# Silu as one ScalarE activation in the first layer's gate of a retention and two-layer feed-forward kernel

## The chip, the cores and the metric

One Trainium2 chip, one of its cores. The metric is the device time of one execution of the whole program, in microseconds (us), given as the median of the runs. Five engines matter: TensorE (PE in the profile, with its weight loads as PEld), VectorE (DVE), ScalarE (ACT), GpSimd (POOL) and SyncE (SP, which here issues DMAs). Each engine works through its own queue in order. An instruction that has to wait for another engine holds up all that stands behind it in its queue.

## The reference, cut to what matters

Retention over 4 batches of 8 heads (576 positions, 64 dimensions a head) gives 2304 tokens of 512 values. Two feed-forward layers follow. Each has a hidden width of 2048, and everything is float32.

```python
def _moe_ref(x, w_in, w_out):            # first layer, "layer 0"
    h = x @ w_in                         # (2304, 512) @ (512, 2048)
    g = h * (1.0 / (1.0 + np.exp(-h)))   # the gate: silu(h)
    return (g @ w_out).astype(np.float32)

def _moe2_ref(x, w_in, w_out):           # second layer, "layer 1"
    h = x @ w_in
    r = np.maximum(h, 0.0)
    g = r * r
    return (g @ w_out).astype(np.float32)
```

## The kernel before, in words

Every float32 product is made of three fp32r matmuls: each operand is split into a rounded high part and the rest (`xh`/`xl`, `wh`/`wl`, `gh`/`gl`), and `mm3` (line 74) adds high times high, high times low and low times high.

The tokens are cut into five blocks of 512, 384, 384, 512 and 512 (`BLOCKS`). The order of the work is written out by hand. The main loop (lines 504 to 529) goes through 160 steps: layer 0 with its five blocks, then layer 1 with its five blocks, each block in 16 steps `f` of 128 hidden columns. A step `i` emits, in this order:

- `gemm1(i)`: 12 matmuls from `x` and the weights into the PSUM tile `ph` (two buffers). It puts `gate(i)` on the list `later`.
- First half: `conv_to` (weight conversion, below) where weights are still to be converted, and then `flush`, which emits all that stands in `later`. What these emit may put new entries on the list, for the next flush.
- Second half: `conv_to`, `flush`, and then `gemm2(i-2)` (`LAG` is 2): 12 matmuls from `gh`, `gl` and the weights into the four PSUM tiles `acc`.
- After either half in layer 0, at evenly spaced places, a part of the retention of the next block (`scores`, `values`), whose own DVE and ACT work goes onto `later` too.

In the kernel before, the gate of step `i` takes three flushes. First half of step `i`: ACT computes Sigmoid from `ph` into `sg` (line 380), DVE multiplies `ph` by it into `sg` (line 381). Second half of step `i`: ACT rounds `sg` into `gh` (line 388). First half of step `i+1`, behind that half's weight conversion: DVE makes `gl = sg - gh` (line 389). `gemm2(i)` on PE in step `i+2` needs both. Layer 1 has its own gate (lines 383 and 384), with the same split.

The weights come as 512 KB pieces in a 64-bit layout and are converted on the chip: ACT lines 101, 102 (`conv_a`) and 121 (`conv_c`), DVE lines 107 to 109 (`conv_b`) and 125 (`conv_d`). For layer 0 this runs during the start and the 16 steps of block 0, one piece in each half step. For layer 1 it runs from the last block of layer 0 into the first steps of layer 1. After each `conv_b` SP is given the load of a later piece into the buffer that this `conv_b` frees.

Before layer 1 can begin with a block, `load_x2` (lines 435 to 444) loads the first layer's result back (SP), copies it four times on ACT (`xh`, line 442) and subtracts it four times on DVE (`xl`, line 443). The first `load_x2` is emitted at the end of step `f = 8` of the last block of layer 0, the second at the end of step `f = 4` of the first block of layer 1.

Before the start a Sigmoid of one element (`dummy`, line 455) runs on ACT.

Of the kernel before, what the change touches and what calls it, by code (L numbers as in the profile page):

```python
# [9 lines left out]
ACTF = mybir.ActivationFunctionType  # L10
# [28 lines left out]
def kernel(  # L39
# [16 lines left out]
    nc = tc.nc  # L56
# [72 lines left out]
    later = []  # L129
# [44 lines left out]
    dummy = cp.tile([128, 1], F32, name="dummy")  # L174
# [184 lines left out]
    def gemm1(layer, j, f):  # L359
        n = BLOCKS[j]  # L360
        ph = ps_g.tile([128, 512], F32, tag="g", name="ph")[:, 0:n]
        wh, wl = wt[layer, f]
        xh, xl = x_t[j] if layer == 0 else late["x", j]
        for k in range(KD):
            w0 = slice(k * 128, k * 128 + 128)
            mm3(
                ph,
                [(wh[:, w0], xh[:, k, 0:n]), (wh[:, w0], xl[:, k, 0:n]), (wl[:, w0], xh[:, k, 0:n])],
                first=k == 0,
                last=k == KD - 1,  # L370
            )
        later.append(lambda: gate(layer, j, f, ph))

    def gate(layer, j, f, ph):
        n = BLOCKS[j]
        s = gp.tile([128, 512], F32, tag="sg", name="sg", bufs=2)[:, 0:n]
        gh = gp.tile([128, NBMAX], F32R, tag="gh", name="gh")[:, 0:n]
        gl = gp.tile([128, NBMAX], F32R, tag="gl", name="gl")[:, 0:n]
        if layer == 0:
            nc.scalar.activation(s, ph, ACTF.Sigmoid)  # L380
            nc.vector.tensor_mul(s, ph, s)  # L381
        else:
            nc.scalar.activation(s, ph, ACTF.Relu)  # L383
            nc.vector.scalar_tensor_tensor(s, ph, 0.0, s, op0=ALU.max, op1=ALU.mult)  # L384
        g_t[layer, j, f] = (gh, gl)

        def split():
            nc.scalar.copy(gh, s)  # L388
            later.append(lambda: nc.vector.tensor_sub(gl, s, gh))  # L389

        later.append(split)

    def gemm2(layer, j, f):
        n = BLOCKS[j]
# [57 lines left out]
    for _ in range(WARM):  # L452
        mm(warm[:, 0, 0:256], zero[:, 0:128], zero[:, 0:256], start=True, stop=True)
    nc.vector.memset(dummy, 0.0)
    nc.scalar.activation(dummy, dummy, ACTF.Sigmoid)
    for u in range(n_start):
        if u == 0:
            new_raw(u)
# [45 lines left out]
    for i in range(len(seq) + LAG):  # L504
        if i < len(seq):
            layer, j, f = seq[i]
# [79 lines left out]
```

## Time and profile before

| | us |
|---|---|
| median of 3 runs | 898.37 (897.97 to 899.33) |
| the profiled execution | 897.14 |
| its span, first to last instruction | 895.40 |
| PE busy | 862.8 (96%) |
| DVE busy | 427.6 (48%) |
| ACT busy | 327.1 (37%) |
| POOL busy | 72.8 (8%) |
| mean granted clock of PE | 0.982 of full speed |

The profile is one execution, so its times are compared with 897.14, of which 1.74 lie outside the span. Busy shares are means over stages that have different limits. The start (about 0 to 40 us) prepares the first block. Block 0 of layer 0 follows, to about 145, then the other blocks of layer 0, to about 490, and layer 1 to the end. An idle engine costs time only where PE waits for it or where the end of the program does.

### The profile page before, as it was taken

The page shows a single profiled execution, that of the slowest core. Times are in us where ns is not written, and L with a number is a line of the kernel's source. Part 1 is how long each engine was busy: PE and PEld are TensorE (multiplying, and loading weights), DVE is VectorE, ACT ScalarE, POOL GpSimd, SP SyncE. Part 2 cuts the span into 40 slices and gives each one's busy share as a digit, 9 for nine tenths or more (in the row PEclk, how much of TensorE's full clock was granted, in tenths as well). Part 3 has the DMA queues.
Part 4 walks back from the last instruction along what each step waited for, and adds up shares of the span by engine and source line. Part 5 has one row for each costly group of instructions (what it writes and reads, how often), then busy time and mean ns, then how long its engine had stood idle before and what let it go on. Part 6 is the DMA issues. An engine that isn't in the chain of part 4 may idle for free.

```text
span 895.4 us, 14028 instructions
## 1 busy us (share of the span) xinstructions
PE 862.8 (96%) x5930; PEld 739.8 (83%) x5930; DVE 427.6 (48%) x722; ACT 327.1 (37%) x594; POOL 72.8 (8%) x105
## 2 busy tenths in 40 slices
PE   6698979999999999999999989999999999999998
PEld 5576758999999888888878878889999888888886
DVE  3899995333443333335767776632242233223222
ACT  3576663222222322225556555432232223222221
POOL 5210111111122021100000000000000000000000
PEclk8699999999999999999999999999999999999999
DMA  9445532111211213002343433020020020001001
GB/s 355 175 140 191 181 127 95 48 48 48 84 49 48 84 48 118 1 1 95 120 139 118 142 131 115 2 83 1 1 83 1 0 83 1 1 0 48 1 1 47
DMA packets 21662, 68.27 MB, mean 76 GB/s; under 512 B 2400, under 2 KB 4192, under 8 KB 21216
## 3 DMA queue, kind: packets, MB, share of 16 engines
q1 hardware_dynamic: 17280, 59.91, 19.5%
q10 hardware_dynamic: 4320, 7.47, 2.3%
q8 instruction: 46, 0.75, 0.3%
q14 instruction: 16, 0.13, 0.0%
HBM read 57.93 MB, written 9.44 MB: 75 GB/s over the span
## 4 chain that ended last, share of the span: by engine, by line
PE 82%; DVE 2%; DMA 1%; issue 0%; ACT 0%; SPq 0%; ACTq 0%
PE acc L74 40%; PE ph L74 39%; PE Q L301 2%; DMA xr<-x 1%; PE P L250 1%; PE P L255 1%; DVE xl L443 0%; DVE t L108 0%; DVE gl L389 0%; DVE t L109 0%; DVE t L107 0%; DVE wl L125 0%; PE Q L317 0%; ACT xh L442 0%; SPq L92 0%
## 5 line engine op out<-in xcount | busy, mean ns | idle before, releaser
L74 PE MATMUL ph<-xh,wh 128*128 128x512 f32 (+1 forms) x640 | 238.1, 372 | 5.6 <-ACT xh L335 5.6
L74 PE MATMUL ph<-xl,wh 128*128 128x512 f32 (+1 forms) x640 | 236.4, 369 | 0.0
L74 PE MATMUL ph<-xh,wl 128*128 128x512 f32 (+1 forms) x640 | 236.3, 369 | 0.0
L384 DVE SCALAR_TENSOR_TENSOR sg<-ph,sg 128x512 f32<-128x512 f32 (+1 forms) x80 | 51.0, 638 | 195.3 <-ACT sg L383 195.3
L74 PEld LDWEIGHTS ph<-xh,wh 128*128 128x128 f32 x640 | 120.8, 189 | 24.0 <-ACT xh L335 5.8
L74 PEld LDWEIGHTS ph<-xl,wh 128*128 128x128 f32 x640 | 120.7, 189 | 16.8 <-DVE xl L336 0.4
L74 PEld LDWEIGHTS ph<-xh,wl 128*128 128x128 f32 x640 | 120.7, 189 | 15.2
L74 PE MATMUL acc<-gl,wh 128*128 128x512 f32 (+1 forms) x320 | 120.2, 376 | 9.6 <-DVE gl L389 9.4
L389 DVE TENSOR_TENSOR gl<-sg,gh 128x512 fp32r<-128x512 f32 (+1 forms) x160 | 103.5, 647 | 52.9 <-ACT gh L388 52.6
L388 ACT CAST gh<-sg 128x512 fp32r<-128x512 f32 (+1 forms) x160 | 92.3, 577 | 91.2 <-DVE sg L384 51.5
L381 DVE TENSOR_TENSOR sg<-ph,sg 128x512 f32<-128x512 f32 (+1 forms) x80 | 50.9, 636 | 148.7 <-ACT sg L380 148.7
L74 PE MATMUL acc<-gh,wh 128*128 128x512 f32 (+1 forms) x320 | 120.5, 377 | 0.0
L383 ACT ACTIVATE sg<-ph 128x512 f32<-128x512 f32 (+1 forms) x80 | 44.5, 556 | 207.9 <-PE ph L74 207.5
L74 PE MATMUL acc<-gh,wl 128*128 128x512 f32 (+1 forms) x320 | 119.0, 372 | 0.0
L74 PE MATMUL acc<-wh,gl 128*128 128x512 f32 x288 | 112.8, 392 | 2.8 <-DVE gl L389 2.8
L74 PE MATMUL acc<-wl,gh 128*128 128x512 f32 x288 | 112.6, 391 | 0.0
L74 PE MATMUL acc<-wh,gh 128*128 128x512 f32 x288 | 112.0, 389 | 0.0
L380 ACT ACTIVATE sg<-ph 128x512 f32<-128x512 f32 (+1 forms) x80 | 44.3, 554 | 159.0 <-PE ph L74 159.0
L74 PEld LDWEIGHTS acc<-gl,wh 128*128 128x128 f32 x320 | 60.8, 190 | 21.3 <-DVE gl L389 13.9
L74 PEld LDWEIGHTS acc<-gh,wh 128*128 128x128 f32 x320 | 60.6, 189 | 8.7
L74 PEld LDWEIGHTS acc<-gh,wl 128*128 128x128 f32 x320 | 60.9, 190 | 7.4
L74 PEld LDWEIGHTS acc<-wh,gl 128*128 128x128 f32 x288 | 54.1, 188 | 14.6 <-DVE gl L389 3.2
(50 smaller groups left out, 738.0 us busy)
## 6 DMA issues: line engine op xcount, KB each, us to landing
wr<-w SPq DMA_DIRECT2D x64, 512.0 KB, 3.5
raw<-att SPq DMA_DIRECT2D x34, 512.0 KB, 5.3
x<-y ACTq DMA_DIRECT2D x12, 256.0 KB, 2.5
xr<-x SPq DMA_DIRECT2D x3, 1024.0 KB, 5.5
out<-y SPq DMA_DIRECT2D x10, 256.0 KB, 2.1
out<-y ACTq DMA_DIRECT2D x7, 256.0 KB, 2.3
x<-y ACTq DMA_DIRECT2D x8, 192.0 KB, 1.9
xr<-x SPq DMA_DIRECT2D x2, 768.0 KB, 5.3
```

Source lines behind the costliest of these rows:

```text
L74: mm(o, a, b, start=first and i == 0, stop=last and i == n - 1)
L250: mm(o, dims(u, a, e, b, 768), dims(u, a, e, b, 0), start=True, stop=True)
L255: mm(o, toks(u, a, e, b, 256), toks(u, a, e, b, 512), start=True, stop=True)
L301: mm(w, a, b, start=e not in started, stop=last)
L380: nc.scalar.activation(s, ph, ACTF.Sigmoid)
L381: nc.vector.tensor_mul(s, ph, s)
L383: nc.scalar.activation(s, ph, ACTF.Relu)
L384: nc.vector.scalar_tensor_tensor(s, ph, 0.0, s, op0=ALU.max, op1=ALU.mult)
L388: nc.scalar.copy(gh, s)
L389: later.append(lambda: nc.vector.tensor_sub(gl, s, gh))
```

## The change

The gate of layer 0 loses its product on DVE. ACT's activation from `ph` into `sg` is Silu in place of Sigmoid. `split` is called at once in layer 0, so that the rounding into `gh` stands directly behind the Silu in ACT's queue, and the subtraction that makes `gl` goes out with the next flush (second half of step `i`) and not with the one after that. Layer 1's gate is as it was. The one-element activation before the start is Silu too.

```diff
         if layer == 0:
-            nc.scalar.activation(s, ph, ACTF.Sigmoid)
-            nc.vector.tensor_mul(s, ph, s)
+            nc.scalar.activation(s, ph, ACTF.Silu)
         else:
             nc.scalar.activation(s, ph, ACTF.Relu)
             nc.vector.scalar_tensor_tensor(s, ph, 0.0, s, op0=ALU.max, op1=ALU.mult)
@@
             nc.scalar.copy(gh, s)
             later.append(lambda: nc.vector.tensor_sub(gl, s, gh))
 
-        later.append(split)
+        if layer == 0:
+            split()
+        else:
+            later.append(split)
@@
     nc.vector.memset(dummy, 0.0)
-    nc.scalar.activation(dummy, dummy, ACTF.Sigmoid)
+    nc.scalar.activation(dummy, dummy, ACTF.Silu)
```

## Rows read from the trace of the kernel before

**Rows 1.** Stretches: busy us (instructions) of each engine, granted clock, DMA share, GB/s.

```profile
40.00:140.00 100.00, 90.16 (x688) 69.98 (x687) 93.75 (x156) 66.43 (x115) 14.99 (x17) 0.98 0.46 153
140.00:450.00 310.00, 310.00 (x2732) 277.68 (x2731) 125.12 (x220) 92.23 (x172) 40.00 (x58) 1.00 0.19 63
450.00:465.00 15.00, 13.13 (x51) 10.37 (x50) 11.05 (x19) 9.39 (x17) 0.00 (x0) 0.89 0.33 114
...
535.00:890.00 355.00, 355.00 (x1649) 304.40 (x1648) 121.40 (x198) 101.99 (x185) 0.00 (x0) 1.00 0.08 27
```

**Rows 2.** PE's waits, 40 to 140: us in total, times, longest us.

```profile
PE acc L74 <- DVE gl L389: 7.5, 8, 2.4
PE Q L301 <- DVE S L286: 2.1, 1, 2.1
```

**Rows 3.** PE's waits from 440 to 540, same columns.

```profile
PE acc L74 <- DVE gl L389: 4.7, 2, 2.8
```

**Rows 4.** DVE, groups by line, 40 to 140: busy us, mean ns; idle before, releaser.

```profile
L381 DVE TENSOR_TENSOR sg<-ph,sg 128x512 f32<-128x512 f32 x15 | 10.2, 682 | 3.0 <-ACT sg L380 3.0
L389 DVE TENSOR_TENSOR gl<-sg,gh 128x512 fp32r<-128x512 f32 x14 | 10.1, 721 | 0.0
```

**Rows 5.** DVE's timeline in block 0: start us, us, instruction.

```profile
54.11 0.68 DVE L381 TENSOR_TENSOR sg<-ph,sg 128x512 f32<-128x512 f32 x1
54.71 0.68 DVE L257 TENSOR_TENSOR rf<-P,cs 128x512 f32<-128x512 f32 x1
...
93.73 0.42 DVE L107 TENSOR_SCALAR t<-t 128x512 int32<-128x512 int32 x1
...
133.18 0.41 DVE L286 TENSOR_TENSOR S<-P,dS 128x256 f32<-128x256 f32 x1
```

**Rows 6.** PE's timeline in block 0, idle time before in brackets.

```profile
83.86 0.50 PE L74 MATMUL acc<-gl,wh 128*128 128x512 f32 x1 [2.38 <-DVE gl L389]
...
84.67 0.60 PE L74 MATMUL acc<-gl,wh 128*128 128x512 f32 x1
...
88.31 0.40 PE L74 MATMUL ph<-xl,wh 128*128 128x512 f32 x1
...
90.84 0.39 PE L74 MATMUL acc<-gh,wh 128*128 128x512 f32 x1
...
97.15 0.50 PE L74 MATMUL acc<-gl,wh 128*128 128x512 f32 x1 [0.48 <-DVE gl L389]
...
133.74 1.09 PE L301 MATMUL Q<-raw,S 64*64 64x64 f32 x30 [2.08 <-DVE S L286]
```

**Rows 7.** ACT's timeline around the first load_x2.

```profile
443.31 0.60 ACT L380 ACTIVATE sg<-ph 128x512 f32<-128x512 f32 x1 [1.80 <-PE ph L74]
...
452.44 2.18 ACT L442 CAST xh<-xr 128x512 fp32r<-128x512 f32 x4 [6.38 <-DMA xr<-x]
```

**Rows 8.** DVE's timeline there.

```profile
453.09 2.50 DVE L443 TENSOR_TENSOR xl<-xr,xh 128x512 fp32r<-128x512 f32 x4 [6.07 <-ACT xh L442]
455.51 0.68 DVE L389 TENSOR_TENSOR gl<-sg,gh 128x512 fp32r<-128x512 f32 x1
...
459.10 0.68 DVE L389 TENSOR_TENSOR gl<-sg,gh 128x512 fp32r<-128x512 f32 x1
```

**Rows 9.** PE's timeline there.

```profile
456.24 0.50 PE L74 MATMUL acc<-gl,wh 128*128 128x512 f32 x1 [1.87 <-DVE gl L389]
...
456.58 0.48 PE L74 MATMUL acc<-gh,wl 128*128 128x512 f32 x1
...
460.23 0.39 PE L74 MATMUL acc<-gh,wl 128*128 128x512 f32 x1
```

**Rows 10.** ACT, groups by line, 40 to 140, columns as in rows 4.

```profile
L101 ACT ACTIVATE t<-wr 128x512 f32<-128x512 f32 x26 | 17.5, 675 | 4.9 <-DMA wr<-w 2.2 <-DVE gl L389 1.7 <-DVE wl L125 1.0
...
L121 ACT CAST wh<-t 128x512 fp32r<-128x512 f32 x28 | 17.4, 621 | 18.6 <-DVE t L109 18.3
...
L380 ACT ACTIVATE sg<-ph 128x512 f32<-128x512 f32 x15 | 8.8, 590 | 1.2 <-PE ph L74 1.2
```

**Rows 11.** ACT's only table load in the whole span, by line.

```profile
L455 ACT ACT_TABLE_LOAD x1 | 1.3, 1283 | 0.7 <-PEq L576 0.7
```

## The prediction

> **What bounds the kernel now.** I read the busy times by stretch first, to see where PE is not full. From 140 to 450 and from 535 to 890 it is busy all the time at full clock [rows 1]. Nothing that DVE or ACT save there can move the end. In the 100 us from 40 to 140, block 0 of layer 0, PE is busy for 90.2 while DVE is busy for 93.8: DVE converts a piece of the weights in each half step and makes the gates between. ACT has 66.4 there. PE's waits in that stretch, read next, are 7.5 us in eight waits for `gl` and 2.1 in one for the retention's state `S`, all made by DVE [rows 2]. The third view is PE's waits around the two `load_x2`: 4.7 us in two waits for `gl`, one of 1.9 at 456 and one of 2.8 [rows 3, 9]. So what can be won is some 14 us in places that can be named, and in each of them PE waits for DVE.
>
> A wait costs more than its length where the granted clock falls behind it. After the 2.38 us wait that ends at 83.86, nine matmuls from 84.67 to 88.31 take 3.64 us, 0.40 each, and from 88.31 to 90.84 eleven take 2.53, 0.23 each [rows 6]: the lower level of 1.2 GHz cost 1.6 us. After the wait at 456.24 nine matmuls take 3.65 us (456.58 to 460.23) [rows 9], again 1.6 too much, and that stretch has a mean clock of 0.89 [rows 1].
>
> **The change part by part.** *The product goes.* One product holds DVE's queue for 0.60 us (from 54.11 to 54.71, where the next one starts) [rows 5], though it is listed at 0.68. From 40 to 140 there are 15 [rows 4]. Two come after the `S` that ends PE's last wait (133.18), 13 before it: 13 x 0.60 = 7.8 us. In addition DVE sat idle for 3.0 us in front of products, until the Sigmoid was there [rows 4]. Of that I take back 2.2: in the two places where a retention copy stands ahead of the gate on ACT, DVE's next `wl` waits for ACT's `wh`, which now stands behind Silu and `gh`, and I leave 0.4 for each. So DVE reaches this `S` 7.8 + 2.2 = 10.0 us earlier, and PE could begin the matmuls behind it at 133.7 - 10.0 = 123.7 [rows 6]. PE alone, without its waits (7.5 + 2.1) and without the slow 1.6, would be there at 133.7 - 11.2 = 122.5. The later one decides: block 0 gives 10.0, with 7.8 (none of the idle time comes back) and 11.2 as its ends.
>
> *Does `gl` still hold PE up?* It leaves with the second half's flush, so it no longer stands behind the next half's conversion. The tightest place that I find is step 7. There the conversion that stood ahead of `gl` begins at 93.73 [rows 5]; `gl` now takes that place, 8 x 0.60 earlier for eight products and 1.4 for the idle time up to there: 87.5, done at 88.2. PE, had it not waited, would want it at 97.15 less the gl waits up to there (0.4, 0.3, 0.9, 0.3, 2.4 and 0.5, of which rows 6 show the two last) and 1.6 of clock, at 90.7. That leaves 2.5 us, so these eight waits go, and the clock's fall behind the 2.38 with them.
>
> *Silu in Sigmoid's place.* No row shows Silu. The nearest is Sigmoid in the same place, 590 ns; the costliest activation of the same size there is the one of line 101, 675 ns, from SBUF [rows 10]. I take 590. The ends are nothing below it (the operands and the size stay) and 675, which is 15 x 0.085 = 1.3 us on an engine that has 33.6 us free in that stretch [rows 1], hidden.
>
> *`gh` is moved forward on ACT*, directly behind the Silu. It no longer waits for a product. What is queued behind it is the second half's `wh` and the first step of the next conversion, which come one cast (616 ns for the same form, near L121's 621 [rows 10]) later; they have waited for DVE 18.3 us in all [rows 10], so that is the cover, and if it is gone DVE's `wl` is late (first rival). No DMA is moved; the weight loads that SP issues after each `conv_b` come earlier with DVE, and no retention load changes its place. In blocks 1 to 4 the same parts are worth nothing, since PE never waits there [rows 1].
>
> *The first `load_x2`.* Its four copies wait for the load until 452.44 on ACT, and its four subtractions until 453.09 on DVE [rows 7, 8]. The `gl` of step 8 stood behind them and came at 455.51 [rows 8]; PE waited 1.87 for it [rows 9]. Now that `gl` is emitted a half step earlier, before `load_x2`, right after the Silu that takes the place of the Sigmoid at 443.31 [rows 7]. It is some nine us early. What is late next is the `gl` of step 9: at 459.10 now [rows 8], less the `gl` and the product that stood between it and the subtractions (2 x 0.60), 457.9, done at 458.6. PE wants it 24 matmuls of 0.23 after 454.4 (456.24 - 1.87), at 459.9. So this wait goes with its slow clock: 1.9 + 1.6 = 3.5, and if the clock falls there anyway, 1.9. The second `load_x2` lies in layer 1, whose gate is not touched: its 2.8 stays.
>
> **The sum.** 10.0 + 3.5 = 13.5 us off the profiled execution's 897.1 (span 895.4 and 1.7 outside it). The median of the runs is 1.2 above that execution; taken off the median, 898.4 - 13.5 = 884.9. The ends of this case are 7.8 + 1.9 = 9.7 (888.7) and 11.2 + 3.5 = 14.7 (883.7), and if the second `load_x2` should win its 2.8 too, 880.9.
>
> **The rivals.** *The saving is eaten by the new order on ACT.* `wh` of the second half now waits for PE's `ph`, for Silu and for `gh`; DVE's `wl` waits for it, and everything of DVE behind that. If this takes 0.6 a step, DVE runs block 0 at its old pace, and all that is left is that `gl` goes out one conversion earlier (93.73 to about 96.4, as PE was released at 97.15 [rows 5, 6], 2.7 us), at most once over the block. With the 3.5 of `load_x2` that is 3.5 to 6.2, about 893.5. For it: DVE and PE have nearly the same amount of work (90 each after the change), so waits on either side add. Against it: ACT is free a third of the time, and by the places worked out above PE is the one that runs ahead.
>
> *Slower: table loads on ACT.* The trace has one table load, 1283 ns, before the first Sigmoid, and none between Sigmoid and the other functions of ACT [rows 11]. If Silu could not share a table with the Abs of line 101, each step of block 0 would need two loads, 28 in the 14 steps of the stretch: 35.9 us. ACT would have 66.4 + 35.9 = 102.3 us of work where PE and DVE have about 90, and with half of its 18.3 us of waits for DVE kept, 111.5. That is 11.5 more than now; less the 3.5 of `load_x2`, about 906. It decides from more than (90 - 66.4) / 14 = 1.7 us of loads a step, so one load a step would be hidden and two are not. Against it: Sigmoid, Abs, Copy and Relu ran here on one load. The Trainium skill, "ScalarE: Activation LUTs", section "Table sets: the hidden batching unit", speaks of this danger: functions come in sets around one costly function, and each change of set is a load. It also says that relu, copy and abs are in every set as filler. The trace agrees for Sigmoid's set; no run here shows Silu's. The page prices a switch at 2.66 us with a drain that no row here shows; an estimate by that would put 74 us on ACT, some 41 us of them beyond the present stretch, about 940.
>
> *No change.* The waits for `gl` turn into waits for other things of DVE, `S` above all, and the clock falls at the same places. This would need DVE not to gain by work that it no longer has. About 898. That Silu is made of two ACT instructions, so that the change isn't what it says, would put 15 x 0.59 = 8.9 us on ACT, 75 of about 90: hidden, the forecast's time.
>
> **How the numbers follow.** Forecast (881 to 889) 0.72; eaten on ACT (889 to 896) 0.17; no change 0.05; slower 0.06. Faster by over 0.2% (1.8 us, about what a measurement of this kernel can tell from none) is 0.72 + 0.17 = 0.89, same 0.05, slower 0.06. The range goes from 881.5, which leaves a little of the forecast's far end out, to 893.5, the middle of the first rival.
>
> **What would show it.** In the changed profile: DVE without line 381's product, some 10 us less busy in block 0; one table load; Silu near 590 ns; PE's waits for `gl` in block 0 near nothing and one of 1 us or so for `S`, its matmuls of `values` begun near 124; no low clock near 85; at the first `load_x2` no wait for `gl`, at the second still 2.8. The prediction is wrong if ACT shows more than one table load, if PE's waits for `gl` in block 0 stay above 4 us in all, or if a wait for `wl` or `wh` appears that was not there.

## The result, and the profile after

The changed kernel takes 888.83 us (median of four executions, 887.45 to 890.08), beside 898.85 (897.97 to 899.37) for the one before: a ratio of 0.9889, with a 95% interval of 0.9869 to 0.9909. That is 10.0 us off, where 13.5 were forecast. It ends inside the stated range, 3.9 us above the predicted time.

The profiled execution is the longest of the four: 890.08 us, span 888.3. It is 7.06 us under the profiled execution before (897.14), so an account made from the two traces has to come to 7.1 and not to 10.0. The four executions lie in two groups, two at 887.5 to 888.0 with a mean granted clock of 0.988 and 0.990, two at 889.7 to 890.1 with 0.983. The profiled one is of the second group, and below it can be seen where its clock falls.

The stretches of the changed kernel (columns as in rows 1):

```profile
40.00:140.00 100.00, 92.92 (x711) 75.30 (x710) 88.90 (x145) 68.38 (x119) 15.12 (x17) 0.97 0.45 154
140.00:450.00 310.00, 310.00 (x2730) 277.53 (x2730) 92.51 (x166) 95.78 (x178) 37.56 (x58) 1.00 0.19 65
450.00:465.00 15.00, 15.00 (x67) 12.40 (x67) 11.95 (x21) 10.71 (x19) 0.00 (x0) 1.00 0.44 140
```

PE's waits from 36 to 136 (us in total, times, longest), against [rows 2], and then from 430 to 540, against [rows 3]:

```profile
PE ph L74 <- ACT xh L335: 6.4, 1, 6.4
PE Q L301 <- DVE S L286: 4.7, 2, 4.1
PE ph L74 <- ACT sg L380: 1.9, 2, 1.3
PE acc L74 <- DVE gl L388: 0.4, 1, 0.4
...
PE acc L74 <- DVE gl L388: 2.7, 1, 2.7
```

The first row is the wait for the block's first operand, ahead of the first matmul of block 0; it belongs to the start and was there before too. In block 0 the eight waits for `gl`, 7.5 us, have become one of 0.4. The wait for `S` has grown from 2.1 to 4.1 (with a small second one 4.7), and two waits of a new kind stand there, for the Silu that frees `ph`, the PSUM tile that `gemm1` writes. At the first `load_x2` nothing is left. At the second the wait is 2.7, as it was.

PE's timeline where the last wait of block 0 ends:

```profile
126.77 1.51 PE L301 MATMUL Q<-raw,S 64*64 64x64 f32 x23 [4.07 <-DVE S L286]
...
129.52 0.79 PE L74 MATMUL acc<-gh,wh 128*128 128x512 f32 x1
...
132.13 0.39 PE L74 MATMUL acc<-gh,wh 128*128 128x512 f32 x1
```

From 129.52 to 132.13 six matmuls take 2.61 us, 0.43 each, where 0.23 is usual: PE is at 1.2 GHz behind this wait (the stretch's granted clock is 0.51, below), as it was behind the one of [rows 6] that ends at 83.86. The matmuls of `values` in front of them take 2.75 us (126.77 to 129.52). From 126.77 to 132.13 that is 5.36 us together; in the kernel before, the same matmuls took 3.04, from 133.74 [rows 6] to here:

```profile
136.78 0.39 PE L74 MATMUL acc<-gh,wh 128*128 128x512 f32 x1
```

So the low clock behind this wait costs 2.3 us.

The granted clock of this stretch (columns as in rows 1):

```profile
125.00:130.00 5.00, 3.23 (x65) 3.15 (x66) 4.84 (x8) 1.66 (x4) 2.76 (x3) 0.51 0.00 0
```

Each kernel's first matmul of block 0, before and after:

```profile
35.23 0.80 PE L74 MATMUL ph<-xh,wh 128*128 128x512 f32 x1 [5.58 <-ACT xh L335]
```

```profile
35.98 0.79 PE L74 MATMUL ph<-xh,wh 128*128 128x512 f32 x1 [6.40 <-ACT xh L335]
```

So the account of the two profiled executions is this. The start was 0.75 longer; in the second run of the same kernel (below) block 0 began at 35.34, so that is not the change's doing. From the first matmul of block 0 to the `values` behind the last `S` PE took 98.5 us before (35.23 to 133.74 [rows 6]) and takes 90.8 now (35.98 to 126.77): 7.7 won. The low clock behind it gives 2.3 back. The first `load_x2` wins 1.9 of wait and 1.6 of clock. The second loses 1.4, as the experiment there shows. That makes 7.7 + 3.5 - 0.75 - 2.3 - 1.4 = 6.8 of the 7.06; the rest is in no row that was read.

### The profile page after: what moved, and what is told of

Same layout as the page of the kernel before. It is cut to its first block, busy times and chain, and to the rows that moved or that the text cites. A ratio compares the mean times of both kernels' runs of the same rounds, so it can differ in the third digit from the quotient of the medians.

```text
span 888.3 us, 13947 instructions
## 1 busy us (share of the span) xinstructions
PE 860.0 (97%) x5930; PEld 741.0 (83%) x5930; DVE 381.0 (43%) x642; ACT 327.9 (37%) x594; POOL 70.5 (8%) x105
## 4 chain that ended last, share of the span: by engine, by line
PE 84%; DVE 1%; DMA 1%; ACT 0%; issue 0%; SPq 0%; ACTq 0%
PE acc L74 41%; PE ph L74 40%; PE Q L301 2%; PE P L250 1%; PE P L255 1%; DMA xr<-x 1%; DVE xl L445 0%; PE Q L317 0%; DVE t L108 0%; DVE t L109 0%; DVE t L107 0%; DVE wl L125 0%; DVE gl L388 0%; ACT sg L382 0%; ACT xh L444 0%
## 5 line engine op out<-in xcount | busy, mean ns | idle before, releaser
L74 PE MATMUL acc<-gl,wh 128*128 128x512 f32 (+1 forms) x320 | 118.2, 369 | 0.4 <-DVE gl L388 0.4
L74 PEld LDWEIGHTS acc<-wh,gl 128*128 128x128 f32 x288 | 54.4, 189 | 14.6 <-DVE gl L388 3.2
L74 PEld LDWEIGHTS acc<-wh,gh 128*128 128x128 f32 x288 | 54.5, 189 | 10.5
```

The source lines that it names most:

```text
L74: mm(o, a, b, start=first and i == 0, stop=last and i == n - 1)
```

## The experiments

All of them were timed beside the kernel before, in two groups on two chips. The changed kernel's second run, the late split, the early split alone and the two states in one flush shared 898.25 us for it; the two table loads, `gl` twice and the two with the early split in layer 1 shared 898.44. Where one of the second group is set against the changed kernel's 888.82, that goes across the groups; the ratios to the kernel before give the same differences within 0.3 us.

**The changed kernel once more.**

> The changed kernel as it is, for the comparisons of this group, and to see how much its time moves between executions: 887 to 890 us. Theory (DVE's work up to the last state S sets block 0): the wait of PE for S of about 4 us near 127 is there again. Rival (it was an accident of one execution): it is under 1 us.

Measured: 888.82 us (887.70 to 890.07), ratio 0.9894, interval 0.9880 to 0.9908. The wait for `S` in its trace is 4.07 us again, so it is no accident of one execution.

**Silu alone, the split where it was.** From the changed kernel:

```diff
-        if layer == 0:
-            split()
-        else:
-            later.append(split)
+        later.append(split)
```

> Silu in place of Sigmoid and product, but the split where it was before (gh in the second half, gl in the next step). Theory (block 0 is won by the work taken off DVE, the first load_x2 by gl's earlier place): block 0 wins what the changed kernel wins there, the last S starts near 126, and the first load_x2 keeps its wait of 1.9 us, with or without 1.6 us of slow clock: 1.9 to 3.5 us behind the changed kernel, 890.5 to 892.5. Rival (the earlier place of gl does it all): 896 to 898.5, waits for gl in block 0 as before.

Measured: 887.42 us (885.74 to 888.06), ratio 0.9875, interval 0.9862 to 0.9889. That is 1.4 under the changed kernel in the same group; the two intervals overlap, so it is not shown to be faster, but it is clearly not slower, and my theory had 2 to 3.5 us more. The rival's 896 to 898.5 is off as well. PE's waits of this kernel, 36 to 140 and then 400 to 540:

```profile
PE acc L74 <- DVE gl L388: 3.5, 6, 1.0
PE Q L301 <- DVE S L286: 1.6, 1, 1.6
...
PE acc L74 <- DVE gl L388: 2.9, 1, 2.9
```

Block 0 wins as much as in the changed kernel: from the first matmul to the `values` behind the last `S` it takes 90.34 us. Its waits are many and short where those of the changed kernel are one long one, and no low clock follows them. The surprise is the second stretch. Its one wait is that of the second `load_x2`; the wait at the first is gone, although `gl` of step 8 still stands behind the subtractions there. How, its timelines show: SP's issue of the load, ACT's Silu of step 8, and DVE.

```profile
435.18 0.36 SPq L437 DMA_DIRECT2D xr<-x  x1
```

```profile
435.14 0.60 ACT L380 ACTIVATE sg<-ph 128x512 f32<-128x512 f32 x1 [2.53 <-PE ph L74]
```

```profile
441.42 2.50 DVE L442 TENSOR_TENSOR xl<-xr,xh 128x512 fp32r<-128x512 f32 x4 [4.45 <-ACT xh L441]
443.83 0.68 DVE L388 TENSOR_TENSOR gl<-sg,gh 128x512 fp32r<-128x512 f32 x1
```

Against the kernel before, where SP's issue is

```profile
446.92 0.38 SPq L438 DMA_DIRECT2D xr<-x  x1
```

and the Sigmoid of step 8 starts at 443.31 [rows 7]: the load used to leave 3.6 us after that Sigmoid began, and leaves 0.04 us after the Silu began here. It stands in SP's queue behind a weight load that waits for a `conv_b` of DVE, and DVE no longer waits for the gate before that `conv_b`. The load, the subtractions and `gl` come so much earlier that PE no longer waits.

**The early split alone.** From the kernel before, Sigmoid and product kept:

```diff
-        later.append(split)
+        if layer == 0:
+            split()
+        else:
+            later.append(split)
```

> Sigmoid and the product on DVE stay, and the split alone comes early (gh directly behind the product, gl in the second half). Theory: DVE has all its work up to the last S, so S starts near 133 as before and block 0 wins under 2 us; the first load_x2 loses its wait: 893 to 896. Rival (order alone): 888 to 891. In either case ACT, with gh queued ahead of the second half's wh, now waits for DVE's product; if that costs, the last S comes later than 133.

Measured: 895.37 us (894.53 to 897.54), ratio 0.9966, interval 0.9952 to 0.9979, as my theory had it. PE's waits, 36 to 140 and then 400 to 540:

```profile
PE ph L74 <- DVE sg L381: 5.7, 5, 2.5
...
PE Q L301 <- DVE S L286: 4.7, 2, 4.0
...
PE acc L74 <- DVE gl L389: 2.9, 1, 2.9
```

The waits for `gl` in block 0 are gone here too, but waits of about the same size in all for the product (it frees `ph`) and for `S` stand in their place, and block 0 takes 97.8 us from the first matmul to the `values`, 0.7 less than before. The wait at the first `load_x2` is gone, this time because `gl` of step 8 leaves ahead of the subtractions; the load itself leaves as late as ever, 3.6 us after the Sigmoid of step 8. So there are two causes, and either of them alone removes that wait.

**Two table loads a step.** From the changed kernel:

```diff
         if layer == 0:
             split()
+            if j == 0:
+                nc.scalar.activation(dummy, dummy, ACTF.Sigmoid)
```

> The changed kernel with a Sigmoid of one element behind each gh in block 0 of layer 0, so that Silu's table has to be loaded again in every step of that block: if the two functions lie in two tables, 2 loads a step, 32 more in all at 1.28 us, 41 us of ACT's time. Theory (the slower rival's price): ACT becomes what bounds block 0, as the prediction worked it out, and the kernel ends near 906 (900 to 915), slower than the one before. Rival (ACT's waits for DVE, 16 us in block 0, take most of the loads up): 889 to 897. If one table holds both functions, there are no more loads and nothing changes.

Measured: 904.62 us (903.63 to 907.48), ratio 1.0071, interval 1.0048 to 1.0095: 15.8 us slower than the changed kernel, and within 1.4 us of the 906 that the prediction gave this rival. ACT's groups (busy us, mean ns), and the wait of DVE that the loads make:

```profile
L393 ACT ACT_TABLE_LOAD x16 | 20.5, 1283 | 0.3
L380 ACT ACT_TABLE_LOAD x16 | 20.5, 1283 | 0.3
```

```profile
DVE wl L125 <- ACT wh L121: 17.4, 13, 3.2
```

Silu and Sigmoid lie in different tables, a change between them is 1283 ns each time, and 32 of them, 41 us of ACT's time, cost the kernel 15.8. ACT is busy for 97.1 of the 104 us from 36 to 140, and its wait for DVE's conversion is down to 0.8. In the changed kernel ACT runs Silu, Abs, Copy and Relu on one load, so this rival did not come true; its price came out, if not by its working: block 0 takes 107.6 us from the first matmul to the `values`, 9.0 more than before, where the price had 11.5, with half of ACT's 18.3 us of waits for DVE's conversions kept. ACT's timeline in this run shows what one change costs:

```profile
64.52 0.62 ACT L387 CAST gh<-sg 128x512 fp32r<-128x512 f32 x1
65.16 1.28 ACT L393 ACT_TABLE_LOAD   x1
66.45 0.20 ACT L393 ACTIVATE dummy<-dummy 128x1 f32<-128x1 f32 x1
```

The load begins 0.02 us after the cast ends, and the activation 0.01 after the load: 1.3 us in all. The Trainium skill, "ScalarE: Activation LUTs", section "Table sets: the hidden batching unit", says that relu, copy and abs are in every set; the one load of the changed kernel agrees for Silu's. Its price of 2.66 us with a drain, in the section "What ACT_TABLE_LOAD costs", is not what these rows show; the 1283 ns of the load itself is.

**The two states in one flush.** From the changed kernel:

```diff
             new_state(u, 0, P)
-            later.append(lambda: new_state(u, 1, P))
+            new_state(u, 1, P)
```

> The changed kernel, with both states of a retention step made in one flush on DVE, so that the second S no longer stands behind a weight conversion of 2.5 to 3 us; DVE waits about 0.7 to 1 us for POOL's dS between the two. Theory (S is what PE waits for last in block 0): the wait of 4.1 us before the matmuls of values near 127 shrinks to 0.5 to 2, and the slow clock behind it goes: 2 to 5 us faster than the changed kernel, 884 to 887. Rival (DVE's total work sets the pace, so any wait saved for S comes back as a wait for gl): within 1 us of the changed kernel.

Measured: 888.01 us (887.04 to 888.16), ratio 0.9882, interval 0.9869 to 0.9896. It is 0.8 under the changed kernel, too little to tell apart: the rival's time and not the theory's, though the rival's mechanism is hardly seen (the waits for `gl` are 0.8 us in all, where they were 0.4). PE's waits from 36 to 140:

```profile
PE Q L301 <- DVE S L286: 2.2, 1, 2.2
PE ph L74 <- ACT sg L380: 2.1, 2, 1.8
PE acc L74 <- DVE gl L388: 0.8, 2, 0.5
```

The wait for `S` is half as long, but the low clock follows it all the same. The granted clock is 0.50 from 127 to 130, and the matmuls of `values` take 2.71 us, as in the changed kernel (2.75); only the matmuls behind them are spared, all but the first:

```profile
126.86 1.82 PE L301 MATMUL Q<-raw,S 64*64 64x64 f32 x30 [2.21 <-DVE S L286]
...
129.57 0.79 PE L74 MATMUL acc<-gh,wh 128*128 128x512 f32 x1
```

And DVE now waits twice in block 0 for POOL's `dS`, 1.5 us in all, beside the 0.6 for `wh` that it waited before, and block 0 gains only 1.3 (89.4 us). In this profile the first matmul of block 0 starts at 37.43, 2.1 later than in the run of the changed kernel beside it (35.34); the edit acts in the start too, and PE waits 2.46 us there for an `S`, until 29.71, where the run beside it waits 0.56, until 26.55. That the edit does this was not tried by itself. An earlier place for `S` alone moves the wait more than the time.

**DVE's time put back, without a wait.** From the changed kernel:

```diff
             later.append(lambda: nc.vector.tensor_sub(gl, s, gh))
+            if layer == 0 and j == 0:
+                later.append(lambda: nc.vector.tensor_sub(gl, s, gh))
```

> The changed kernel with the subtraction that makes gl done twice in block 0 of layer 0, the second with the same result: DVE gets back 0.60 us a step, 13 x 0.60 = 7.8 us up to the last S, with no wait for ACT in it. Theory (DVE's work up to the last S sets block 0): S starts 7 to 8 us later, near 133, and the kernel takes 894 to 898. Rival (what was won is the handshake between ACT and DVE, not DVE's time): within 2 us of the changed kernel, 888 to 891.

Measured: 897.48 us (897.08 to 900.12), ratio 0.9993, interval 0.9979 to 1.0008: 8.7 us slower than the changed kernel, and no longer told from the kernel before. PE's waits from 36 to 150:

```profile
PE Q L301 <- DVE S L286: 5.4, 2, 4.8
PE acc L74 <- DVE gl L390: 4.7, 6, 1.2
PE ph L74 <- ACT sg L380: 3.5, 2, 1.7
```

From the first matmul to the `values` block 0 takes 100.2 us. DVE's timeline shows what was put back:

```profile
65.53 0.68 DVE L388 TENSOR_TENSOR gl<-sg,gh 128x512 fp32r<-128x512 f32 x1
66.24 0.69 DVE L390 TENSOR_TENSOR gl<-sg,gh 128x512 fp32r<-128x512 f32 x1
```

The second subtraction, which writes the tile of the first, starts 0.72 us behind it and not 0.60. The 13 of them up to the last `S` are 9.3 us of DVE's queue where 7.8 were meant, and block 0 is 9.4 longer than in the changed kernel (90.8); the theory had 7 to 8. The order of the change, its single ACT operation and its lack of a handshake are all there, and without DVE's time they win nothing in block 0, which is 1.6 longer than before. So what the change wins in block 0 is DVE's time.

**The early split in layer 1 too.** From the changed kernel:

```diff
-        if layer == 0:
-            split()
-        else:
-            later.append(split)
+        split()
```

> The changed kernel with the split called at once in layer 1 too, so that the gl of the step before the second load_x2 leaves ahead of its subtractions. Theory: PE's wait of 2.7 to 2.9 us near 518 goes, with or without 1.5 us of slow clock behind it, and nothing else changes: 1.5 to 4.5 us faster than the changed kernel, 884.5 to 887.5. Rival: ACT, whose gh now waits for DVE's product directly, loses it elsewhere, or the gl of the next step takes the wait's place: within 1 us, 888 to 889.5.

Measured: 885.88 us (885.44 to 886.46), ratio 0.9862, interval 0.9834 to 0.9889: 2.9 under the changed kernel. The executions of the two (887.45 the changed kernel's fastest) do not overlap, though the intervals of their ratios do, just. PE's only wait from 400 to 560:

```profile
PE ph L74 <- DVE sg L383: 0.5, 1, 0.5
```

The changed kernel has this there:

```profile
517.99 0.80 PE L74 MATMUL acc<-wh,gl 128*128 128x512 f32 x1 [2.73 <-DVE gl L388]
518.58 0.63 PE L74 MATMUL acc<-wh,gh 128*128 128x512 f32 x1
...
521.13 0.40 PE L74 MATMUL acc<-wh,gh 128*128 128x512 f32 x1
```

Behind its 2.73 us the clock is low: six matmuls from 518.58 to 521.13 take 2.55 us and not 1.4, and with the one at 517.99 that is 1.4 us. In the kernel before no low clock followed the wait of 2.83 at this place, which is the 1.4 that the account above gives back.

**Silu with the late split, and the early split in layer 1.** From the changed kernel:

```diff
-        if layer == 0:
+        if layer == 1:
             split()
         else:
             later.append(split)
```

> Silu with the late split in layer 0 (as in the run that did so) and the early split in layer 1. Theory: the two add, the run with the late split (887.4) less 1.5 to 4.5 us: 883 to 886, the fastest so far. Rival (no gain in layer 1): 887 to 888.

Measured: 883.85 us (883.69 to 884.07), ratio 0.9837, interval 0.9814 to 0.9860. This is the fastest version, 5.0 us under the changed kernel and 14.6 under the kernel before. Both effects add, and with no wait over 1.6 us left in these places, its four executions lie within 0.4 us, where those of the changed kernel spread over 2.4.

## Why the prediction was right, and where it was not

*The time: in the range, in part by luck.* The medians' 10.0 us lies in the case's own 9.7 to 14.7, near its lower end; the 7.1 of the two profiled executions does not. Two losses that no sum held, 2.3 us of low clock behind `S` and 1.4 at the second `load_x2`, are in the profiled one, and the two shorter executions, by which the median comes out lower, were not profiled.

*The product's time: right.* 13 slots of 0.60 us went. The idle time in front of the products was to shrink by 2.2; from 3.0 [rows 4] it went to 0.65, the waits for `wh` that stand in its place, by 2.3. The run with `gl` twice shows the same from the other side: 9.3 us put back, 9.4 lost.

*Block 0's sum of 10.0: too large by 2.3.* `S` came at 126.20 and not at 123.2 (0.75 of that is the later start). DVE's way to it, from its first conversion in block 0 to the last `S`, is

```profile
35.82 0.42 DVE L107 TENSOR_SCALAR t<-t 128x512 int32<-128x512 int32 x1
```

before, up to 133.18 [rows 5]: 97.4 us. After, it is

```profile
36.57 0.42 DVE L107 TENSOR_SCALAR t<-t 128x512 int32<-128x512 int32 x1
...
126.20 0.42 DVE L286 TENSOR_TENSOR S<-P,dS 128x256 f32<-128x256 f32 x1
```

89.6 us. That is 7.7 less, while 7.8 + 2.3 = 10.1 had gone. The other 2.4 is conversions that became longer, which the sum held constant. Over the 28 pieces on that way the time from the start of line 107 to the next start adds up to 15.6 us and not 14.0, and that of line 108 to 22.5 and not 21.3; `gl` gives 0.8 of these 2.8 back, and the rest adds some 0.4. DVE's timeline of the kernel before, behind the two lines of [rows 5] at 54.11 and 54.71, shows the first:

```profile
55.30 0.41 DVE L107 TENSOR_SCALAR t<-t 128x512 int32<-128x512 int32 x1
55.75 0.69 DVE L108 CUSTOM_DVE_ANT_0 t<-wr,t 128x1024 uint16<-128x1024 uint16 x1
...
57.69 0.42 DVE L107 TENSOR_SCALAR t<-t 128x512 int32<-128x512 int32 x1
58.24 0.69 DVE L108 CUSTOM_DVE_ANT_0 t<-wr,t 128x1024 uint16<-128x1024 uint16 x1
```

Line 108 follows line 107 after 0.45 us where the product has come shortly before, and after 0.55 elsewhere. In the changed kernel it is 0.55 nearly everywhere, as here:

```profile
57.12 0.42 DVE L107 TENSOR_SCALAR t<-t 128x512 int32<-128x512 int32 x1
57.66 0.69 DVE L108 CUSTOM_DVE_ANT_0 t<-wr,t 128x1024 uint16<-128x1024 uint16 x1
```

Line 108 reads what ACT's line 102 made. The short step goes with the product and not with the order: behind the first piece, 11 of the other 27 have it in the kernel before and 11 in the run with the early split alone, but none in the changed kernel and none in the run with Silu and the late split. A likely reading is that the product's own wait for the Sigmoid, which stands behind line 102 on ACT, had covered line 108's wait; that is argued from the order, and no run takes it by itself. The second part is conversions that run while POOL does: line 108 takes 0.89 us or more seven times on that way instead of four, and line 107 once 0.95. Each of these overlaps an instruction of POOL in its trace; why they meet more often was not looked into. DVE's groups from 36 to 138, before and then after (busy us, mean ns):

```profile
L108 DVE CUSTOM_DVE_ANT_0 t<-wr,t 128x1024 uint16<-128x1024 uint16 x29 | 21.4, 737 | 2.2
L107 DVE TENSOR_SCALAR t<-t 128x512 int32<-128x512 int32 x29 | 12.3, 423 | 0.0
```

```profile
L108 DVE CUSTOM_DVE_ANT_0 t<-wr,t 128x1024 uint16<-128x1024 uint16 x29 | 22.4, 772 | 3.5
...
L125 DVE TENSOR_TENSOR wl<-t,wh 128x512 fp32r<-128x512 f32 x30 | 21.8, 726 | 0.6 <-ACT wh L121 0.6
L107 DVE TENSOR_SCALAR t<-t 128x512 int32<-128x512 int32 x29 | 12.7, 438 | 0.1
```

*PE's own arrival at 122.5: too late.* PE stood ready 4.07 us before 126.77, at 122.7, though it had lost 3.0 in four short waits up to there and had begun 0.75 later. Without them it would have been there at 119.7, or 118.9 with the start of before: 3.6 us ahead of the working. The step subtracted only the waits, and the one low clock, that the profile names. Delays too short to be listed as waits went too: set against 0.2275 us from one start to the next at full clock, they were 4.8 us up to there before and are 2.1 now. And the low clock at the block's start cost 2.0 us and not 2.6; why is not shown. So the wait for `S` was 4.1 and not about 1, and the low clock behind it, 2.3 us in the profiled execution, was in no sum.

*`gl` in block 0: right.* 0.4 us is left, at 90.03. But the early place was not needed for it as much as I wrote: with the late split the six waits are 3.5 us in all, and the time is no worse.

*The first `load_x2`: right in size (1.9 + 1.6), wrong in its cause.* The step put it down to `gl` leaving before the subtractions. That is enough, as the early split alone shows. It is not necessary: Silu with the late split removes the wait as well, since DVE no longer waits for the Sigmoid ahead of the `conv_b` on which SP's queue, and in it the load, depends. The prediction named this queue ("come earlier with DVE") and did not follow it to `load_x2`.

*Silu: right.* It takes 592 ns in the mean for 128x512 where Sigmoid took 595, and there is one table load. *The second `load_x2`: its wait stayed*, 2.7, as written.

*`gh` directly behind Silu: no `wl` became late to speak of.* DVE waits for `wh` in block 0 twice, 0.3 us each, which it did not before; that is one of the prediction's signs of being wrong, but its own sum had left 0.4 for each of the two. So the first rival, 0.6 a step, is out. What became late was the Silu itself, twice, behind the retention's copy on ACT, with `ph` to free: 1.9 us that the working did not have.

## What to carry to other kernels

Taking work off an engine is worth its queue time where that engine sets the pace, and nothing where PE is full: 80 products went, 46.6 us of DVE's 427.6, and only the 13 of block 0 that lie ahead of the last state paid, with the one stall at a load. Ask of a removed wait whose queue stood behind it: DVE's wait for the Sigmoid had also delayed SP's loads. And when a sum holds two engines that come out nearly equal, check both for small gaps that move with the edit: here the next wait was 4.1 us where their difference gave about 1.

## What was not expected of the hardware

The low clock behind a wait is not regular. In the kernel before, a wait of 2.38 us was followed by it at 83.86 [rows 6], and one of the same length at 120.04 was not, nor was the 2.08 at 133.74; the 1.87 at 456.24 was [rows 9], and so was the 2.21 in the run with the states together. At the second `load_x2`, the same place with a wait of 2.7 to 3.0 us in eight of the traces, it followed in four (the changed kernel, its second run, the late split, the early split alone) and not in the other four. Behind the late split it lasted longest there, with a granted clock of 0.50 from 514 to 520. What decides between the two is not shown.

The version without a wait over 1.6 us in these places repeats within 0.4 us, so such waits may cost spread as well as time. With four executions of each that is not shown: the run with the early split in both layers still has its 4.1 us wait for `S` and repeats within 1.0.
